# A two-stage attention and ELU kernel, rewritten: row 4p+j on partition p, fp32 loads cast on chip, one activation table, two-bank PSUM tiles, a fixed order of instructions

## Chip, cores, metric

One core of a Trainium2 chip. The metric is the device time of one execution in microseconds (us). A run has several executions, and its median is quoted. A few executions are slower (over 1.5% above the fastest of the same kernel); the ratios leave them out. The engines are PE (TensorE, the matrix engine; PEld is its weight load), DVE (VectorE), ACT (ScalarE), POOL (GpSimd) and SP (the queue engine that issues most transfers).

## The reference

```python
def _attn_ref(q, k, v, g_norm):                       # q, k, v: 8 x 8 heads x 576 x 64
    kv = np.einsum('bhsd,bhse->bhde', k, v)
    out = np.einsum('bhsd,bhde->bhse', q, kv)
    rms = np.sqrt(np.mean(out * out, axis=-1, keepdims=True) + 1e-06)
    return (out / rms * g_norm).astype(np.float32)

def _moe_ref(x, w_in, w_out):                         # x: 4608 x 512, w_in: 512 x 2048
    h = x @ w_in
    g = np.where(h > 0.0, h, np.exp(np.minimum(h, 0.0)) - 1.0)    # ELU
    return (g @ w_out).astype(np.float32)

# reference: attention, then x = heads side by side as (batch*seq, 512), then _moe_ref
```

Two large products, 4608 x 512 x 2048 and 4608 x 2048 x 512, do nearly all the arithmetic. In pieces of 128 x 128 weights and 512 moving columns they are 576 matmuls each, 1152 together. Attention is about 600 small matmuls and a row-wise norm.

## The kernel before

bf16 compute throughout. PE writes its results to tiles in a memory called PSUM; a tile of 128 x 512 fp32 is called one bank here. The software queue on POOL loads fp32 data and casts it in flight. Attention works on chunks of 128 tokens. The norm is exp(-0.5 ln(mean square + eps)) on ScalarE, and ELU is max(h, min(exp(h), 1) - 1). The compiler's scheduler orders the instructions of each engine. The parts that the argument touches:

```python
# ... one-bank PSUM tiles for both products, two of each ...
warm = const.tile([1, 1], FP32, name="warm")
nc.scalar.activation(warm, warm, AF.Exp)
nc.scalar.activation(warm, warm, AF.Ln, bias=1.0)

def load_qkv(b):                       # 128 rows a piece; runs of 64 elements
    for c in range(NCH):
        for name, src in (("k", k), ("v", v), ("q", q)):
            nc.gpsimd.dma_start(out=tiles[name][0:rows, c, :, :],
                in_=src[b, :, c*P : c*P+rows, :].rearrange("h p d -> p h d"))

def attn_chunks(b):                    # 36 chunks of 128 tokens in all
    for g in chunks:
        # ... four to eight matmuls into se_ps ...
        nc.scalar.activation(sq, se_ps, AF.Square)
        nc.vector.reduce_sum(out=ss, in_=sq, axis=X)
        nc.scalar.activation(ss, ss, AF.Ln, bias=eps_col, scale=1.0 / D)     # L185
        nc.scalar.activation(ss, ss, AF.Exp, scale=-0.5)                     # L186
        nc.vector.tensor_tensor(out=xs, in0=se_ps, in1=ss.to_broadcast(...), op=mult)
        # ... four transposes on PE, a copy to xT ...

def mlp_mm1(T):                        # T: 512 tokens
    for f in range(FC):                # 16
        # ... four matmuls into h_ps (128 x 512, one bank) ...
        nc.scalar.activation(e, h_ps, AF.Exp)                                # L222
        nc.vector.tensor_scalar(out=e, in0=e, scalar1=1.0, scalar2=1.0, op0=min, op1=subtract)
        nc.vector.tensor_tensor(out=gT[:, f, :], in0=e, in1=h_ps, op=max)    # L226

for T in range(NT):                    # 9
    # ... load, attn_pairs and attn_chunks of batch T + 2 ...
    mlp_mm1(T)
    if T > 0: mlp_mm2(T - 1)
```

## Time and profile before

442.52 us, the median of 3 runs (442.22 to 445.96).

The head of the profile page of the kernel before (span; busy time and share of each engine), then its chain that ended last, by engine and by line. The chain runs backwards from the last instruction, at each step to whatever released it:

```profile
span 442.4 us, 4765 instructions
PE 343.1 (78%) x1743; PEld 160.1 (36%) x1776; DVE 199.5 (45%) x408; ACT 265.9 (60%) x451; POOL 105.1 (24%) x128
...
PE 54%; ACT 34%; DVE 5%; POOL 3%; issue 2%; DMA 1%; ACTq 0%; POOLq 0%; DVEq 0%
PE h_ps L214 22%; PE o_ps L234 21%; ACT L185 10%; ACT L186 9%; ACT elu_e L222 5%; PE ps_shared L128 4%; PE qt_ps L147 3%; ACT sq L182 3%; DVE xs L189 2%; ACT ss L185 2%; PE ps_shared L197 2%; ACT xT L204 2%; ACT L222 2%; PE se_ps L173 2%; ACT ss L186 1%
```

PE is busy for 78% of the span (33 of its 1776 matmuls are missing from this trace: x1743 beside 1776 weight loads), yet the chain runs through it for only 54%. "ACT L185" and "ACT L186" without a tile's name are not the Ln and the Exp (those carry the name ss) but the activation-table loads ahead of them. The costliest groups of the same kernel (engine, operation, out<-in, shapes, count | busy us, mean ns of one | idle time before them):

```profile
L222 ACT ACTIVATE elu_e<-h_ps 128x512 bf16<-128x512 f32 x144 | 85.8, 596 | 77.6 <-PE h_ps L214 66.9
L226 DVE TENSOR_TENSOR gT<-elu_e,h_ps 128x512 bf16<-128x512 bf16 x144 | 98.5, 686 | 4.1
...
L185 ACT ACT_TABLE_LOAD x35 | 44.9, 1283 | 0.6
...
L186 ACT ACT_TABLE_LOAD x30 | 38.5, 1283 | 0.5
```

With six more at L222 and two at the start there are 73 loads, 73 x 1.283 = 93.7 us. Busy time by window in the kernel before (columns: length; busy us and instructions of PE, PEld, DVE, ACT and POOL; the granted TensorE clock, as a share of full speed; DMA share; GB/s):

```profile
0.00:50.00 50.00, 19.69 (x117) 10.76 (x119) 12.86 (x25) 24.80 (x43) 35.92 (x45) 1.00 1.64 155
50.00:150.00 100.00, 72.41 (x408) 35.48 (x415) 48.35 (x97) 81.48 (x139) 44.09 (x53) 0.83 1.27 82
150.00:350.00 200.00, 165.45 (x847) 76.58 (x862) 102.45 (x211) 128.20 (x217) 25.14 (x30) 0.91 0.34 39
350.00:442.00 92.00, 85.57 (x378) 37.26 (x384) 35.84 (x77) 31.47 (x53) 0.00 (x0) 0.99 0.12 46
```

From 50 to 150 us ScalarE is the busiest engine (81 of 100) and PE works at 0.83 of its clock. PE is dense at full clock only when attention is over: its last transposes start at 318.74 us, and from 319 to 350 us PE is busy for 30.7 of 31 us at a clock of 1.00. (The last window also holds the end, where PE has nothing left to do.) One chunk's norm, from the timeline of the kernel before (start us, length us, engine, line, operation):

```profile
54.98 1.28 ACT L185 ACT_TABLE_LOAD   x1
...
56.28 0.30 ACT L185 ACTIVATE ss<-ss,eps_col 128x8 f32<-128x8 f32 x1
56.60 1.28 ACT L186 ACT_TABLE_LOAD   x1
...
57.89 0.21 ACT L186 ACTIVATE ss<-ss 128x8 f32<-128x8 f32 x1
...
58.13 0.69 DVE L189 TENSOR_TENSOR xs<-se_ps,ss 128x512 bf16<-128x512 f32 x1 [2.40 <-ACT ss L186]
...
58.88 0.40 PE L197 MATMUL ps_shared<-ident,xs 128*128 128x128 bf16 x4 [2.18 <-DVE xs L189]
```

Two loads stand inside one norm: 2.57 of the 3.15 us from the first load's start to the multiply. The brackets say that VectorE stood idle for 2.40 us before its multiply, waiting for the Exp, and PE for 2.18 us before its transposes, waiting for the multiply.

### The profile page before, as it was taken

The numbers are of one execution on the slowest core, as the hardware profiler recorded it, in microseconds if no ns is written. First come the engines' busy times: TensorE is split into PE (matmuls) and PEld (weight loads), VectorE is DVE, ScalarE is ACT, GpSimd is POOL, SyncE is SP. The second block draws the span as 40 slices with busy tenths as digits, with TensorE's granted clock in tenths as the row PEclk, the third lists the DMA queues.
The fourth block names the chain that finished last, engine by engine and source line by source line (L and its number), as shares of the span: only waits on it lengthen the run. The fifth ranks groups of instructions, "written<-read, shape, count | busy, mean of one in ns | idle before, by whom it ended". The sixth has DMA issues, their size and how long they took to land.

```text
span 442.4 us, 4765 instructions
## 1 busy us (share of the span) xinstructions
PE 343.1 (78%) x1743; PEld 160.1 (36%) x1776; DVE 199.5 (45%) x408; ACT 265.9 (60%) x451; POOL 105.1 (24%) x128
## 2 busy tenths in 40 slices
PE   0443955956758947995699759995799999999994
PEld 0221422423323523452244423442344444444441
DVE  0051644643336744634564436544573636626400
ACT  2186699796797687439953894369843434424311
POOL 9949394470740280009100000000000000000000
PEclk9999988966878979999899978996899999999999
DMA  9999999590990490029600200020002002020022
GB/s 92 175 175 155 180 147 101 34 128 1 72 88 2 109 144 4 0 96 119 41 2 18 78 0 0 1 96 0 1 1 95 1 0 96 0 96 1 0 97 95
DMA packets 120040, 28.11 MB, mean 64 GB/s; under 512 B 112848, under 2 KB 114896, under 8 KB 120016
## 3 DMA queue, kind: packets, MB, share of 16 engines
q0 software_dynamic: 115104, 18.36, 59.1%
q1 hardware_dynamic: 4912, 9.44, 5.7%
q8 instruction: 14, 0.23, 0.2%
q14 instruction: 10, 0.08, 0.1%
HBM read 36.70 MB, written 9.44 MB: 104 GB/s over the span
## 4 chain that ended last, share of the span: by engine, by line
PE 54%; ACT 34%; DVE 5%; POOL 3%; issue 2%; DMA 1%; ACTq 0%; POOLq 0%; DVEq 0%
PE h_ps L214 22%; PE o_ps L234 21%; ACT L185 10%; ACT L186 9%; ACT elu_e L222 5%; PE ps_shared L128 4%; PE qt_ps L147 3%; ACT sq L182 3%; DVE xs L189 2%; ACT ss L185 2%; PE ps_shared L197 2%; ACT xT L204 2%; ACT L222 2%; PE se_ps L173 2%; ACT ss L186 1%
## 5 line engine op out<-in xcount | busy, mean ns | idle before, releaser
L214 PE MATMUL h_ps<-xT,w_in_sb 128*128 128x512 bf16 x560 | 158.4, 407 | 2.8 <-DVE gT L226 1.5
L234 PE MATMUL o_ps<-w_out_sb,gT 128*128 128x512 bf16 x559 | 149.3, 395 | 4.1 <-ACT o_sb L242 3.1
L222 ACT ACTIVATE elu_e<-h_ps 128x512 bf16<-128x512 f32 x144 | 85.8, 596 | 77.6 <-PE h_ps L214 66.9
L226 DVE TENSOR_TENSOR gT<-elu_e,h_ps 128x512 bf16<-128x512 bf16 x144 | 98.5, 686 | 4.1
L214 PEld LDWEIGHTS <-w_in_sb 128*128 128x128 bf16 x576 | 58.0, 104 | 77.3 <-issue 33.5
L234 PEld LDWEIGHTS <-gT 128*128 128x128 bf16 x576 | 57.5, 102 | 66.1 <-issue 8.0
L223 DVE TENSOR_SCALAR elu_e<-elu_e 128x512 bf16<-128x512 bf16 x144 | 42.8, 304 | 83.4 <-ACT elu_e L222 83.2
L197 PE MATMUL ps_shared<-ident,xs 128*128 128x128 bf16 x144 | 17.5, 258 | 68.0 <-DVE xs L189 51.6
L189 DVE TENSOR_TENSOR xs<-se_ps,ss 128x512 bf16<-128x512 f32 x36 | 24.8, 690 | 72.9 <-ACT ss L186 72.9
L114 POOL DMA_DIRECT2D k_sb<-in_k_dram x40 | 36.2, 906 | 90.1 <-PE ps_shared L128 54.7
L242 ACT COPY o_sb<-o_ps 128x512 f32<-128x512 f32 x31 | 18.1, 585 | 45.9 <-PE o_ps L234 43.1
L185 ACT ACT_TABLE_LOAD x35 | 44.9, 1283 | 0.6
L197 PEld LDWEIGHTS <-xs 128*128 128x128 bf16 x144 | 10.5, 111 | 87.7 <-DVE xs L189 86.6
L114 POOL DMA_DIRECT2D v_sb<-in_v_dram x40 | 36.1, 902 | 15.3 <-DMA w_out_sb<-in_moe_w_out_dram 8.2
L186 ACT ACT_TABLE_LOAD x30 | 38.5, 1283 | 0.5
L114 POOL DMA_DIRECT2D q_sb<-in_q_dram x40 | 38.3, 957 | 0.2
L128 PE MATMUL ps_shared<-v_sb,k_sb 128*128 128x128 bf16 (+1 forms) x160 | 20.9, 242 | 12.9 <-DMA v_sb<-in_v_dram 11.6
L137 ACT CAST bd_kv<-ps_shared 64x64 bf16<-64x64 f32 x46 | 9.5, 206 | 29.6 <-PE ps_shared L128 26.5
L184 DVE TENSOR_REDUCE ss<-sq 128x8 f32<-128x512 bf16 x36 | 23.8, 680 | 5.7 <-ACT sq L182 5.1
L147 PE MATMUL qt_ps<-ident,q_sb 128*128 128x128 bf16 (+1 forms) x160 | 21.2, 236 | 4.9 <-DMA q_sb<-in_q_dram 4.1
L173 PE MATMUL se_ps<-bd_kv,qT_sb 128*128 128x128 bf16 (+1 forms) x160 | 23.1, 259 | 0.5 <-ACT qT_sb L154 0.4
L204 ACT COPY xT<-ps_shared 128x512 bf16<-128x512 bf16 x31 | 17.9, 579 | 9.2 <-PE ps_shared L197 8.7
(28 smaller groups left out, 122.4 us busy)
## 6 DMA issues: line engine op xcount, KB each, us to landing
out_dram<-o_sb SPq DMA_DIRECT2D x9, 1024.0 KB, 4.3
k_sb<-in_k_dram POOLq DMA_DIRECT2D x32, 128.0 KB, 4.7
v_sb<-in_v_dram POOLq DMA_DIRECT2D x32, 128.0 KB, 4.8
q_sb<-in_q_dram POOLq DMA_DIRECT2D x32, 128.0 KB, 4.9
w_in_sb<-in_moe_w_in_dram POOLq DMA_DIRECT2D x1, 2048.0 KB, 13.2
w_out_sb<-in_moe_w_out_dram POOLq DMA_DIRECT2D x1, 2048.0 KB, 15.3
k_sb<-in_k_dram POOLq DMA_DIRECT2D x8, 64.0 KB, 4.8
v_sb<-in_v_dram POOLq DMA_DIRECT2D x8, 64.0 KB, 4.3
```

Source lines behind the costliest of these rows:

```text
L114: nc.gpsimd.dma_start(out=tiles[name][0:rows, c, :, :], in_=src[b, :, c * P : c * P + rows, :].rearrange("h p d -> p h d"),)
L128: nc.tensor.matmul(kv_ps, lhsT=k_sb[0:rows, c, 2 * p : 2 * p + 2, :], rhs=v_sb[0:rows, c, 2 * p : 2 * p + 2, :], start=(c == 0), stop=(c = ...
L147: nc.tensor.matmul(qt_ps[:, c * P : c * P + rows], lhsT=q_sb[0:rows, c, 2 * p : 2 * p + 2, :], rhs=ident[0:rows, 0:rows], is_transpose=True,)
L185: nc.scalar.activation(ss, ss, AF.Ln, bias=eps_col, scale=1.0 / D)
L186: nc.scalar.activation(ss, ss, AF.Exp, scale=-0.5)
L189: nc.vector.tensor_tensor(out=xs.rearrange("p (h e) -> p h e", h=H), in0=se_ps.rearrange("p (h e) -> p h e", h=H), in1=ss.to_broadcast([P, ...
L197: nc.tensor.matmul(p4_ps[:, j, :], lhsT=xs[:, j * P : j * P + P], rhs=ident, is_transpose=True,)
L214: nc.tensor.matmul(h_ps, lhsT=w_in_sb[:, c, f * P : f * P + P], rhs=xT[:, c, T * 512 : T * 512 + 512], start=(c == 0), stop=(c == KC - 1),)
L222: nc.scalar.activation(e, h_ps, AF.Exp)
L223: nc.vector.tensor_scalar(out=e, in0=e, scalar1=1.0, scalar2=1.0, op0=ALU.min, op1=ALU.subtract)
L226: nc.vector.tensor_tensor(out=gT[:, f, :], in0=e, in1=h_ps, op=ALU.max)
L234: nc.tensor.matmul(o_ps, lhsT=gT[:, f, ts * P : ts * P + P], rhs=w_out_sb[:, f, :], start=(f == 0), stop=(f == FC - 1),)
```

## The change

The intent: put four successive rows on one partition (row 4p+j on partition p), so that loads move runs of 1 KB on the hardware queue, in fp32, and are cast on chip; keep the one table set that holds exp and ln; halve the number of ScalarE and VectorE instructions with tiles two banks wide; and fix the order by hand, so that attention stands between matmuls of both products. The 64 rows left over of each batch of 576 form a ninth group. A cut of the diff:

```diff
+    nc.scalar.preload_act_table_set("natural_log_exp_and_others")
+    ctx.enter_context(tc.manual_schedule())
-    warm = const.tile([1, 1], FP32, name="warm")
-    nc.scalar.activation(warm, warm, AF.Exp)
-    nc.scalar.activation(warm, warm, AF.Ln, bias=1.0)
 # [cut]
+    def fetch_main(name, src, b):
+        st = stage_tile()                                   # fp32, six of them
+        nc.sync.dma_start(
+            out=st.rearrange("p (h x) -> p h x", h=H),
+            in_=src[b, :, 0:G, :].rearrange("h (p j) d -> p h (j d)", j=J))
 # [cut: tails of 64 rows, weights in four slices each; then the casts, 512 columns each, mostly on POOL]
+        def se(h):                                          # half a group: 256 tokens
+                se_ps = at_tile(FP32, 0).rearrange("p (c f) -> p c f", c=2)    # one tile for all of attention
 # [cut: eight matmuls]
+                nc.scalar.activation(sq, se_ps, AF.Square)
+                nc.vector.reduce_sum(out=ss, in_=sq.rearrange("p c (h e) -> p (c h) e", h=H), axis=AX.X)
+                nc.scalar.activation(ss, ss, AF.Ln, bias=eps_col, scale=1.0 / D)
+                nc.scalar.activation(ss, ss, AF.Exp, scale=-0.5)
+                nc.vector.tensor_tensor(out=..., in0=se_ps..., in1=ss.to_broadcast([P, 2 * H, D]), op=ALU.mult)
+        return {0: kv, 1: q_t, 2: se(0), 4: se(1), 6: x_t}  # piece by slot
+    def mm1(T, i):                                          # eight matmuls, two f at once
+        h_ps = ps_m1.tile([P, 2, G], FP32, name="h_ps", tag="mm1")
 # [cut]
+        nc.scalar.activation(e, h_ps, AF.Exp)
 # [cut: min and subtract, max, on 1024 columns, in rest()]
+    cast_all(1)
+    for i in range(8):
+        mm1(0, i)()                                         # group 0: first product alone
+    fetch(2)
+    at = attention(1)
+    for i, n in ((0, None), (1, 1), (2, 0), (3, 2)):        # six of its eight units of the second
+        mm2(0, i)
+        if n is not None:
+            at[n]()
+    mm2(0, 4)
+    at[4]()
+    mm2(0, 5)
+    at[6]()
+    late = [6, 7]
+    for T in range(1, NT):                                  # NT = 9 groups of 512 tokens
 # [cut: casts of T+1, loads of T+2]
+        for i in range(8):
+            rest = mm1(T, i)
+            if T == 1:
+                if i < 2:
+                    mm2(0, late[i])
+            else:
+                mm2(T - 1, i)
+            rest()
+            if T + 1 < NT and i in at:
+                at[i]()
+    for i in range(8):
+        mm2(NT - 1, i)
```

## The prediction

> **What bounds it now.** (1) To about 11 us nothing but loads (busy time by window: PE 1.0 us of 11). (2) 50-150 us: PE busy is 72 of 100 us at a granted clock of 0.80-0.86, ScalarE 81 of 100. The page lists 73 activation-table loads of 1283 ns, 93.7 us; the chain that ended last gives ScalarE 34%, the Ln and Exp lines 18%, nearly all of it table loads. (3) From 350 us PE is dense at clock 1.00: 49 matmuls of 512 columns take 10.74 us on the chain, so 0.216 us each. The 1152 large matmuls are thus worth 248 us at full clock, in a span of 442.
>
> **Removed.** All table loads but one. The Trainium skill (ScalarE: Activation LUTs, "Table sets: the hidden batching unit") says one set holds both exp and ln; this trace shows the alternation and its 1283 ns. Also removed: 115,104 small packets on the software queue, whose issues cost POOL 110 us. Attention: 9 groups of 512 tokens in place of 36 of 128.
>
> **Added.** fp32 loads and on-chip casts. The stores' packets (2 KB) went at 9.44 MB in 5.7% of 442 us, 374 GB/s; for 1-2 KB loads I estimate 250-370 GB/s, so 12-14 us a batch, hidden after the start. POOL casts: no line shows one; from its 128-column memset (205 ns) and select (309 ns) I estimate 0.5-0.9 us per 512 columns, 14 a batch, about 10 us of 33, hidden; at the start 50 of them, 35 us.
>
> **Moved.** ELU on 1024 columns: Exp about 1.03 us, min/sub 0.44 (from 304 ns at 512 and 2343 at 8192), max 1.22; 2.9 us with handoffs. With two buffers, eight matmuls (1.73 us) alone run one pair-tile per 2.3 us, but interleaved with eight of the second product the chain has 3.5 us of slack: PE-bound. Within a group Square-reduce-Ln-Exp-multiply takes about 4.5 us against 6.9 us of matmuls placed between its ends: hidden. ScalarE then works about 17 of 33 us, VectorE 20.
>
> **Sum.** Small matmuls: 60-95 ns start to start in dense stretches at full clock, so 68 a group are about 5 us.
> - Until the first product starts (load q, k, v; one attention alone, serial): 37 us (32-48).
> - First product of group 0, alone: 18.
> - Six units of its second product with attention 1, too little work to hide the chain: 22.
> - Group 1: 26.
> - Groups 2-7: 6 x 33 = 198.
> - Group 8, no attention: 28.
> - Last second product, alone: 14; copy and store: 4.
>
> Total 347 us. PE stays dense, so the clock should rise to about 0.97. The skill (TensorE: Matmul & The Clock Gate, "The HAM clock gate") lets the clock fall after idle windows of about 3.4 us; the trace agrees in direction (0.80 where gaps of 2-4 us lie, 1.00 where dense).
>
> Predicted 347 us, 332 to 369. Chances: faster 0.97, same 0.02, slower 0.01.
>
> **What would show each step.** Table loads: 1. Exp about 1.03 us on 128x1024. PE busy over 95% of each window from group 2 to the end, clock 1.00 there, groups 33 us apart. First large matmul at 32-48 us. Chain of waits: PE over 80%.
>
> **What would make it wrong.** POOL casts twice my estimate (port shared with VectorE) would stall group 1's attention by 10-20 us. Loads at 180 GB/s would add 10-20 us at the start. A chain I call hidden may show: 2 us per group are 14 us. Small matmuls at 150 ns (the cold rate) would add 4 us a group.

## The result

351.97 us, the median of 4 runs (350.18 to 352.89), against 444.24 us before (442.22 to 449.66, 4 runs); the ratio is 0.7903, interval 0.7843 to 0.7962. 449.66 is 1.7% above the fastest, and without it the median is the 442.52 quoted above. A ratio here is the mean time of one kernel's fast runs over that of the other's of the same rounds, so not quite the ratio of the medians quoted.

The page head, the chain and the groups of the changed kernel, to be read against those of before:

```profile
span 351.1 us, 4399 instructions
PE 303.7 (86%) x1760; PEld 151.2 (43%) x1760; DVE 180.8 (52%) x207; ACT 145.9 (42%) x200; POOL 82.3 (23%) x144
...
PE 78%; DVE 8%; ACT 7%; DMA 4%; issue 1%; SPq 1%; DVEq 0%
...
L285 ACT ACTIVATE elu_e<-h_ps 128x1024 bf16<-128x1024 f32 x72 | 73.4, 1021 | 57.2 <-PE h_ps L277 57.2
L291 DVE TENSOR_TENSOR gT<-elu_e,h_ps 128x1024 bf16<-128x1024 bf16 x72 | 87.9, 1221 | 7.5
...
L132 POOL CAST q_bf<-st 128x512 bf16<-128x512 f32 x36 | 21.5, 633 | 138.6 <-DMA st<-in_q_dram 118.9
```

ScalarE's busy time fell by 120 us, of which 72 loads are 92. PE's fell by 39 us although it does the same products. Part of this is the clock: in the mean 0.921 was granted before and 0.982 now.

Busy time by the stages that the prediction had named (start; first product of group 0; six units of its second product with attention 1; group 1; group 2 to the last matmul):

```profile
0.00:36.80 36.80, 9.40 (x68) 6.99 (x69) 10.59 (x15) 7.71 (x14) 16.74 (x34) 1.00 0.98 321
36.80:57.57 20.77, 17.01 (x64) 6.65 (x64) 11.82 (x14) 8.28 (x8) 15.43 (x26) 1.00 1.11 298
57.57:79.52 21.95, 15.82 (x118) 8.53 (x117) 9.32 (x9) 7.45 (x14) 8.17 (x14) 0.99 0.60 165
79.52:111.25 31.73, 27.61 (x148) 12.88 (x148) 17.78 (x20) 13.18 (x19) 14.15 (x24) 0.85 0.57 156
111.25:345.50 234.25, 233.69 (x1364) 116.18 (x1363) 131.33 (x150) 108.73 (x147) 27.77 (x47) 1.00 0.27 83
```

The last line is the point of the rewrite: for 234 us PE is busy for all but 0.6 us at full clock, while VectorE works for 131 and ScalarE for 109. The kv matmuls (k times v, the first matmuls of a batch's attention) of successive batches, from PE's timeline, give the period of a group:

```profile
115.42 2.01 PE L177 MATMUL at<-v_bf,k_bf 128*128 128x128 bf16 x20
...
147.68 2.01 PE L177 MATMUL at<-v_bf,k_bf 128*128 128x128 bf16 x20
```

32.26 us: 128 large matmuls at 0.216 us are 27.6, and the 68 small ones take the other 4.6. Nothing else is left in a group. Of the 47.4 us in which PE is not busy (351.1 - 303.7), 41.4 lie before 111.25 us.

| stage | predicted us | measured us |
|---|---|---|
| to the first large matmul | 37 | 36.8 |
| first product of group 0 | 18 | 20.8 |
| six units with attention 1 | 22 | 22.0 |
| group 1 | 26 | 31.7 |
| groups 2 to 7 (111.25 to 304.02) | 198 | 192.8 |
| group 8 (to 331.66) | 28 | 27.6 |
| last product (to 345.5) | 14 | 13.8 |
| copy, store, end | 4 | 5.6 |
| sum | 347 | 351.1 |

(331.66 is 331.44 us, where the last 65 large matmuls start on the timeline, plus one of 0.216 us.)

### The profile page after: what moved, and what is told of

It is laid out like the page before. It is cut to its first block, busy times and chain, and to the rows that moved or that the text cites. A ratio compares the mean times of both kernels' runs of the same rounds, so it can differ in the third digit from the quotient of the medians.

```text
span 351.1 us, 4399 instructions
## 1 busy us (share of the span) xinstructions
PE 303.7 (86%) x1760; PEld 151.2 (43%) x1760; DVE 180.8 (52%) x207; ACT 145.9 (42%) x200; POOL 82.3 (23%) x144
## 4 chain that ended last, share of the span: by engine, by line
PE 78%; DVE 8%; ACT 7%; DMA 4%; issue 1%; SPq 1%; DVEq 0%
PE h_ps L277 33%; PE o_ps L305 33%; PE at L177 5%; DMA st<-in_v_dram 4%; DVE gT L291 3%; PE at L252 2%; ACT elu_e L285 2%; PE at L210 2%; PE at L192 2%; DVE xs L236 2%; DVE ss L229 2%; DVE elu_e L288 1%; ACT sq L227 1%; ACT xT L262 1%; ACT qT L200 1%
## 5 line engine op out<-in xcount | busy, mean ns | idle before, releaser
L277 PE MATMUL h_ps<-xT,w_in_sb 128*128 128x512 bf16 x576 | 141.7, 390 | 8.8 <-DVE gT L291 5.7
L285 ACT ACTIVATE elu_e<-h_ps 128x1024 bf16<-128x1024 f32 x72 | 73.4, 1021 | 57.2 <-PE h_ps L277 57.2
L291 DVE TENSOR_TENSOR gT<-elu_e,h_ps 128x1024 bf16<-128x1024 bf16 x72 | 87.9, 1221 | 7.5
L288 DVE TENSOR_SCALAR elu_e<-elu_e 128x1024 bf16<-128x1024 bf16 x72 | 34.6, 480 | 93.3 <-ACT elu_e L285 93.1
L132 POOL CAST q_bf<-st 128x512 bf16<-128x512 f32 x36 | 21.5, 633 | 138.6 <-DMA st<-in_q_dram 118.9
L229 DVE TENSOR_REDUCE ss<-sq 128x16 f32<-128x1024 bf16 x18 | 21.9, 1219 | 21.8 <-ACT sq L227 21.8
L236 DVE TENSOR_TENSOR xs<-at,ss 128x1024 bf16<-128x1024 f32 x18 | 22.0, 1225 | 11.3 <-ACT ss L233 11.3
L227 ACT ACTIVATE sq<-at 128x1024 bf16<-128x1024 f32 x18 | 18.5, 1026 | 18.2 <-PE at L210 15.6
L177 PE MATMUL at<-v_bf,k_bf 128*128 128x128 bf16 (+1 forms) x160 | 17.2, 232 | 8.2 <-ACT qT L200 8.2
L132 POOL CAST v_bf<-st 128x512 bf16<-128x512 f32 x28 | 16.9, 641 | 8.4 <-DMA st<-in_v_dram 8.4
L252 PE MATMUL at<-ident,xs 128*128 128x128 bf16 x144 | 10.3, 229 | 6.7 <-DVE xs L236 6.7
```

Source lines behind the costliest of these rows:

```text
L132: eng.tensor_copy(out=out_, in_=in_)
L177: nc.tensor.matmul(kv_ps[:, p, :], lhsT=k_sb[0:rows, c, 2 * p : 2 * p + 2, :], rhs=v_sb[0:rows, c, 2 * p : 2 * p + 2, :], start=(c == 0), ...
L229: nc.vector.reduce_sum(out=ss, in_=sq.rearrange("p c (h e) -> p (c h) e", h=H), axis=AX.X)
L236: nc.vector.tensor_tensor(out=st["xs"][:, 2 * h : 2 * h + 2, :].rearrange("p c (h e) -> p (c h) e", h=H), in0=se_ps.rearrange("p c (h e) - ...
L277: nc.tensor.matmul(h_ps[:, a, :], lhsT=w_in_sb[:, c, f * P : f * P + P], rhs=x[:, c, :], start=(c == 0), stop=(c == KC - 1),)
L291: nc.vector.tensor_tensor(out=gT[T][:, 2 * i : 2 * i + 2, :], in0=e, in1=h_ps, op=ALU.max)
```

## The experiments

A total that fits says nothing about which part of a rewrite earned it. The first eight runs take the parts one at a time; the last four use what came out. All twelve gave correct results. "Before" was run in the same rounds each time (medians 443.99 to 445.2; two of them hold one slow execution). The runs went over four chips: the control, the filled, the one-bank and the scheduler's-order run shared one. The fast medians of before on the four, 442.92 to 444.53 us, lie 1.6 us apart, so a difference between runs on two chips is uncertain by about that much.

| run | median us | ratio to before | interval |
|---|---|---|---|
| changed kernel, control | 351.28 | 0.7912 | 0.7877 to 0.7948 |
| before + one table set | 357.88 | 0.8040 | 0.7998 to 0.8082 |
| changed, two table sets | 359.23 | 0.8088 | 0.8029 to 0.8147 |
| changed, software loads | 365.88 | 0.8223 | 0.8182 to 0.8264 |
| changed, products in blocks | 397.71 | 0.8939 | 0.8897 to 0.8982 |
| changed, gaps filled | 350.22 | 0.7876 | 0.7842 to 0.7910 |
| changed, one-bank tiles | 350.80 | 0.7887 | 0.7845 to 0.7928 |
| changed, scheduler's order | 338.52 | 0.7614 | 0.7572 to 0.7657 |
| scheduler's order, two table sets | 359.08 | 0.8078 | 0.8005 to 0.8151 |
| new opening (3 fast of 4) | 342.59 | 0.7729 | 0.7666 to 0.7792 |
| new opening, shorter start | 338.10 | 0.7621 | 0.7571 to 0.7671 |
| the last, scheduler's order | 331.78 | 0.7470 | 0.7426 to 0.7514 |

### One table set in the kernel before

```diff
-    warm = const.tile([1, 1], FP32, name="warm")
-    nc.vector.memset(warm, 0.0)
-    nc.scalar.activation(warm, warm, AF.Exp)
-    nc.scalar.activation(warm, warm, AF.Ln, bias=1.0)
+    nc.scalar.preload_act_table_set("natural_log_exp_and_others")
```

> The kernel before with the one table set that holds both exp and ln loaded at the start, nothing else changed. Theory A (mine): the 73 loads of 1283 ns were on the chain only in the crowded part, and behind them stands the same schedule, with one-bank tiles whose exp-min-max chain holds PE: table loads fall from 73 to 1, ScalarE's busy time from 266 to about 174 us, the time from 444 to 400-415 us. Rival B: the loads were the whole story: the 18% of the chain goes and the time falls to 355-370 us.

Measured: 357.88 us. Theory A was wrong and the rival right: this one line is worth 86.6 us, and all the rest of the rewrite then adds 6.6 us (357.88 to the control's 351.28). The head of its page:

```profile
span 356.7 us, 4723 instructions
PE 317.1 (89%) x1776; PEld 150.6 (42%) x1776; DVE 200.3 (56%) x407; ACT 172.8 (48%) x377; POOL 105.0 (29%) x128
...
PE 70%; DMA 11%; POOL 7%; DVE 6%; ACT 3%; issue 2%; POOLq 0%; DVEq 0%
```

The chain's share on ScalarE falls from 34% to 3%. The spans of the two profiles differ by 85.7 us (442.4 and 356.7), and they split in two: time in which PE was not busy fell from 99.3 to 39.6 us (442.4 - 343.1 and 356.7 - 317.1), 59.7 us; PE's busy time for the same work fell by 26.0 us, with the granted clock up from 0.921 to 0.998. (The 33 matmuls missing from the trace of before, at 0.216 us each, could move up to 7 us from the first part to the second.) The waits that went are PE's before the transposes of the normalised tile (ps_shared <- ident, xs): for xs and for the copy that empties the tile, they sum to 68.0 us before (51.6 and 16.4) and to 5.8 here (5.0 and 0.8). So the 92.4 us of removed loads (72 x 1.283) paid twice: fewer waits, and fewer slow matmuls. My theory had taken the tiles of one bank for the next limit, and PE is at 49.4 to 49.8 of every 50 us from 100 to 300 us with those tiles.

### Two table sets in the changed kernel

```diff
-    nc.scalar.preload_act_table_set("natural_log_exp_and_others")
```

> The changed kernel without the preload of the joint set, so that Ln and Exp alternate between sets again: about 36 to 55 loads of 1283 ns, 46 to 70 us more on ScalarE. Theory A: the fixed interleave hides nearly all of it from group 2 on (4.4 us of chain in 6.9 us of slack), so group period stays within 1 us of 32.3; the serial parts (start, attention 1, group 1) pay about 2.6 us per half, 6 halves: 366-378 us. Rival B: table loads cost what they take: 398-422 us.

Measured: 359.23 us, 8 us over the control, with 37 loads back. Theory A's mechanism held, its size was too high (it expected 366 to 378). The kv matmuls of successive batches in this kernel:

```profile
120.00 2.01 PE L176 MATMUL at<-v_bf,k_bf 128*128 128x128 bf16 x20
152.26 2.01 PE L176 MATMUL at<-v_bf,k_bf 128*128 128x128 bf16 x20
184.65 2.01 PE L176 MATMUL at<-v_bf,k_bf 128*128 128x128 bf16 x20
```

The period is 32.26 and then 32.39 us, against 32.26: in the steady groups the loads cost next to nothing. The 4.6 us by which the 120.00 lies after the 115.42 of the changed kernel's first profile are paid earlier, where too little stands beside the norm: 1.0 up to the kv matmuls of attention 1 (65.28 against 64.25), 1.0 more up to those of group 1 (88.20 against 86.17) and 2.6 in group 1. That is nearly all of the 5.1 us by which these two profiled executions differ (357.95 and 352.89). The medians, from two chips, differ by 8; what the slower executions pay besides is not shown.

### Scheduler's order, two table sets

```diff
-    ctx.enter_context(tc.manual_schedule())
-    nc.scalar.preload_act_table_set("natural_log_exp_and_others")
```

> The changed kernel with the order left to the scheduler and, besides, without the preload, so that its 36 to 54 table loads are back. It asks why 73 loads cost 87 us in the kernel before and 36 cost 8 us in the changed one. Theory A: the wide tiles do it (half the loads, and chains that are started half as often): 343-352 us, 5 to 13 us over the scheduler's 338.5. Rival B: the fixed order hid them, and a scheduler that does not count on loads lets PE wait for each: 365 us or more.

Measured: 359.08 us, 20.6 us over the same kernel with one set (338.52), between the two theories. From group 3 on, its kv matmuls come every 34.2 us (145.52, 179.69, 213.87, 248.04 us on its timeline) in place of 32.26, so here each group does pay, about 1.9 us. About half is paid before: the 145.52 already lies 10.6 us after the 134.94 of the one-set partner, and the two profiles end 19.9 us apart. Set side by side, what a table load cost in time:

| kernel | loads | their time, us | what they cost, us |
|---|---|---|---|
| before (narrow tiles, scheduler) | 73 against 1 | 92.4 | 86.6 |
| changed, scheduler's order | 37 against 1 | 46.2 | 20.6 |
| changed, fixed order | 37 against 1 | 46.2 | 8.0 |

(The costs are differences of medians; the one-set partners are the run with one table set in the kernel before, the run in the scheduler's order and the control.) The wide tiles halve the number of loads, and what remains costs less per load; the fixed order hides most of it besides. The traces show where the cost lands: the loads add 46.6 us to PE's waits for the normalised tile in the kernel before (51.6 against 5.0), 13.6 in the scheduler's order (23.9 against 10.3) and 5.1 in the fixed order (19.6 against 14.5). Why a load in the kernel before cost nearly its full time is not settled by a run of its own. An estimate from the profile's durations: per 128 tokens the serial norm before is 0.60 + 0.68 + 1.28 + 0.30 + 1.28 + 0.21 + 0.69 = 5.0 us, 36 times 181 us; in wide tiles with the loads 1.03 + 1.22 + 2.57 + 0.31 + 0.22 + 1.22 = 6.6 us, 18 times 118 us. The loads also stand among ELU's Exps on ScalarE's timeline (the Exp at 58.01 us comes after the loads at 54.98 and 56.60). That the crowding does it is argued, not shown; wide tiles and hardware loads came together in this comparison.

### Software loads in the changed kernel

```diff
     def fetch_main(name, src, b):
-        st = stage_tile()
-        nc.sync.dma_start(out=st..., in_=src[b, :, 0:G, :].rearrange("h (p j) d -> p h (j d)", j=J))
+        t = qkvp.tile([P, J + 1, H, D], BF16, name=f"{name}_bf", tag=name)
+        for j in range(J):
+            nc.gpsimd.dma_start(out=t[:, j, :, :],
+                in_=src[b, :, 0:G, :].rearrange("h (p j) d -> p j h d", j=J)[:, j, :, :])
 # the tails likewise; no casts of q, k and v on chip
```

> The changed kernel with q, k and v loaded by the software queue with the cast in flight, as before, into the same tiles; no fp32 staging and no POOL casts of them. Theory A: the load path matters at the start only: one batch takes about 29-32 us of all 16 engines (261 us for 8 batches and the weights in the kernel before), so the first large matmul moves from 37 to about 55-65 us and group 1's and 2's attention wait; the steady groups (32.3 us) just keep up: 375-400 us. Rival B: small packets do not matter once the rest is interleaved: within 2% of 352.

Measured: 365.88 us, 14.6 us over the control. The first large matmul, in this kernel and in the changed one:

```profile
50.86 6.31 PE L280 MATMUL h_ps<-xT,w_in_sb 128*128 128x512 bf16 x16 [0.84 <-DVE xT L262]
```
```profile
36.80 5.99 PE L277 MATMUL h_ps<-xT,w_in_sb 128*128 128x512 bf16 x16 [0.84 <-DVE xT L259]
```

The first large matmul comes 14.1 us later. By the kv matmuls of group 2 the lag is 12.5 us (127.92 against 115.42), so 1.6 us are won back in between; the steady period is again 32.26 us (127.92, 160.18, 192.44 us on its timeline), and the two profiled executions end 12.7 us apart (365.62 and 352.89). So the load path matters at the start alone, as theory A said; its waits in groups 1 and 2 did not come, and its range was too high. "Within 2%" also falls: the two ratios differ by 3.9% and their intervals lie apart.

### Products in blocks

```diff
         for i in range(8):
             rest = mm1(T, i)
-            mm2(T - 1, i)
             rest()
             if T + 1 < NT and i in at:
                 at[i]()
+        for i in range(8):
+            mm2(T - 1, i)
```

(Group 1 is treated likewise with its two units.)

> The changed kernel with both products of a group in blocks: all eight units of the first product (with the attention pieces still between them), then all eight of the second. Theory A: the interleave is what hides the exp-min-max chain: the first product then runs at the rate of group 0's, about 2.5 us a unit in place of 1.73, and the attention chain has half the matmuls to hide behind: 6 to 10 us a group, 400-425 us in all, with PE waiting for VectorE's max and for the normalised tile. Rival B: two-bank tiles with two buffers suffice by themselves: under 360 us.

Measured: 397.71 us, 46 us over the control and 2 us below theory A's range. A group now takes 39.5 us (kv at 150.88, 190.37, 229.92), 7.2 us more than 32.26. PE's timeline shows what it is spent on:

```profile
161.98 1.89 PE L277 MATMUL h_ps<-xT,w_in_sb 128*128 128x512 bf16 x8 [0.38 <-DVE gT L291]
164.96 0.61 PE L210 MATMUL at<-bd_kv,qT 128*128 128x128 bf16 x8 [1.09 <-DVE xs L236]
166.61 3.75 PE L277 MATMUL h_ps<-xT,w_in_sb 128*128 128x512 bf16 x16 [1.05 <-DVE gT L291]
171.45 1.05 PE L252 MATMUL at<-ident,xs 128*128 128x128 bf16 x16 [1.09 <-DVE xs L236]
...
174.83 13.98 PE L305 MATMUL o_ps<-w_out_sb,gT 128*128 128x512 bf16 x64
```

In the first product PE waits again and again, for VectorE's max (gT), which frees a tile, and for the normalised tile (xs); with a wait for the copy of q these add up to 6.1 us in the group from 150.88 us. Then 64 matmuls of the second product run without a gap, when VectorE and ScalarE have little to do. Interleaving the two products is thus necessary in this kernel. It was there before, too, made by the scheduler.

### One-bank tiles

```diff
-    ps_m1 = ... tile_pool(name="ps_m1", bufs=2, ...)    # tiles of two banks
+    ps_m1 = ... tile_pool(name="ps_m1", bufs=4, ...)    # tiles of one bank
+        # Exp, min and subtract, max for each of the two f alone, on 512 columns
```

> The changed kernel with one-bank tiles for the first product (four buffers of one bank, Exp, min/sub and max on 512 columns). Theory A: from group 2 on PE bounds, so more fixed cost on ScalarE (+12 us) and VectorE (+19 us) is hidden; group 0's first product gains from the finer pipeline or loses from VectorE's 8 us: 348-356 us, same within 2%. Rival B: the two-bank tiles carry part of the gain: 362 us or more.

Measured: 350.80 us, the control's 351.28 within the intervals. With one table set and the fixed order, the width of the first product's tiles does not matter; the steady period is 32.26 us here as well. ScalarE is busy for 154.5 us in place of 145.6 and VectorE for 198.7 in place of 181.2, and this is hidden. So this part of the change, halving the instructions of ELU, earned nothing measurable (attention's tiles stayed two banks wide).

### Gaps filled

```diff
     mm2(0, 4)
+    fill(11)          # matmuls of 512 columns into a free tile of the first product
     at[4]()
     mm2(0, 5)
+    fill(11)
     at[6]()
+    fill(4)
```

> The changed kernel with 26 needless large matmuls (their results are never read) put where PE waits in attention 1: 11 before the second half, 11 before the transposes, 4 after. Theory A: the clock fell for group 1 (0.84 granted, eight matmuls in 3.87 us in place of 1.89) because PE idled for about 6 of the 9.5 us before it. With the gaps filled the clock stays at 1.0 there, and group 1 is 2.5 to 3.5 us shorter: 348-350 us, that is 2 to 3.5 us under the control. Rival B: the low clock comes from elsewhere (loads at full rate in that window, or chance): the stretch stays slow and the time is the control's or above it.

Measured: 350.22 us against 351.28, just outside theory A's range and 1.1 us under the control where it had expected 2 to 3.5; the intervals overlap, so the timing alone is unclear. The profiles are not. PE's timeline of the control, at the turn to group 1 and at a later row of group 1, then of the filled kernel (L372 is the filler):

```profile
73.46 0.61 PE L210 MATMUL at<-bd_kv,qT 128*128 128x128 bf16 x8 [2.53 <-DVE xs L236]
73.90 1.89 PE L305 MATMUL o_ps<-w_out_sb,gT 128*128 128x512 bf16 x8
78.28 1.05 PE L252 MATMUL at<-ident,xs 128*128 128x128 bf16 x16 [2.48 <-DVE xs L236]
80.17 3.87 PE L277 MATMUL h_ps<-xT,w_in_sb 128*128 128x512 bf16 x8 [0.84 <-DVE xT L259]
83.83 3.01 PE L305 MATMUL o_ps<-w_out_sb,gT 128*128 128x512 bf16 x8
...
102.42 5.30 PE L277 MATMUL h_ps<-xT,w_in_sb 128*128 128x512 bf16 x16 [1.05 <-DVE gT L291]
```
```profile
75.35 2.54 PE L372 MATMUL f_ps<-xT,w_in_sb 128*128 128x512 bf16 x11
78.00 1.05 PE L252 MATMUL at<-ident,xs 128*128 128x128 bf16 x16
78.89 1.03 PE L372 MATMUL f_ps<-xT,w_in_sb 128*128 128x512 bf16 x4
79.89 0.59 PE L277 MATMUL h_ps<-xT,w_in_sb 128*128 128x512 bf16 x2
81.04 1.46 PE L277 MATMUL h_ps<-xT,w_in_sb 128*128 128x512 bf16 x6 [0.55 <-ACT xT L262]
82.33 1.89 PE L305 MATMUL o_ps<-w_out_sb,gT 128*128 128x512 bf16 x8
```

The long durations (3.87 and 3.01 in place of 1.89; 5.30 for 16, where two rows of eight take 3.96 us in the filled kernel) are gone. The granted clock in group 1 is 1.00 in place of 0.85, and group 1 takes 28.9 us (79.89 to 108.83) in place of 31.5 (80.17 to 111.69). The mean clock of all five filled executions is 0.990 to 1.000, that of the six of the control 0.981 to 0.986. The loads in group 1 were not fewer (172 GB/s against 157), so rival B falls. So the gaps did lower the clock. They explain 2.6 us of group 1's loss; that the rest comes from six units of the first product without the second beside them is argued from PE's waits there (for VectorE's max and for the normalised tile, between 92 and 108 us), not tested.

### Scheduler's order

```diff
-    ctx.enter_context(tc.manual_schedule())
```

> The changed kernel with the order of instructions on each engine left to the compiler's scheduler, as in the kernel before, in place of the fixed order. Theory A: the scheduler works with costs that are not the chip's and bunches small work, as the trace of before shows (large matmuls in blocks of 35 and 49, waits of 2-4 us for the normalised tile): 365-390 us. Rival B: the written order is just what the scheduler finds: within 1% of 352.

Measured: 338.52 us, 12.8 us faster than the control. Both theories fell: the order by hand is the slower one. The kv matmuls of the same batch (4) start at 134.94 us here and at 147.68 in the changed kernel:

```profile
134.94 2.01 PE L175 MATMUL at<-v_bf,k_bf 128*128 128x128 bf16 x20
...
167.20 2.01 PE L175 MATMUL at<-v_bf,k_bf 128*128 128x128 bf16 x20
```

They are 12.7 us apart, and both then follow at 32.26 us, so from there on the two run alike. The whole difference lies before, 10.2 us of it before the kv matmuls of batch 3 (105.22 against 115.42). It is the opening, where the scheduler moved units of group 0's second product into the waits of its first product, and of group 1's into group 1's; the hand-written order had left those waits empty.

### A new opening, by hand

```diff
+    fetch(1)
     for s in range(4):
         fetch_w_out(s)
-    fetch(1)
 # [cut: casts of batch 1 likewise ahead of those of w_out]
-    for i in range(8):
-        mm1(0, i)()
-    # ... six units mm2(0, i) with attention 1 between them ...
+    slot = {0: 1, 2: 0, 3: 2, 5: 4, 7: 6}
+    for i in range(8):
+        mm1(0, i)()
+        if i in slot:
+            at[slot[i]]()                 # attention 1 between the units of the first product
 # [cut: all of mm2(0, i) then stands in group 1, as in any later group]
```

> The changed kernel, fixed order, with another opening: batch 1 is loaded and cast before w_out, attention 1 stands between the units of group 0's first product, and all of group 0's second product stands between the units of group 1's first, as in every later group. Theory A: the loss against the scheduler's order (351 to 338.5 us) lies all in the opening, where attention 1 has too little beside it: large work is moved to where PE waits, group 2 starts at 94-98 us in place of 111, the time is 332-340 us, the granted clock stays at 1.0 after 45 us. Rival B: the opening is bound by the loads (4.2 MB of w_out then come later), and the gaps only move: 345 us or more.

Measured: 342.59 us, the median of its three fast executions (343.08 with the fourth), 8.7 us better than the control and 2.6 us worse than theory A's range. The clock did not stay at 1.0: its mean was 0.986 to 0.990 in the three. The profile that should show where the 2.6 us went fell on the fourth, an odd execution of 1102 us (see the last section), so this run does not tell; the next one's profile does.

The same with a shorter start (the edit is against the run above):

```diff
+        else:                                          # batch 0
+            fetch_tail("k", k, b, nc.scalar)
+            fetch_tail("v", v, b, nc.scalar)
 # [cut]
     cast("k", 0, [V])
+    at0[1]()                                           # transposes of q
     cast("v", 0, [V, A])
 # [cut]
+    at0[4](ps_m1.tile([P, 2, G], FP32, name="h_ps", tag="mm1"))    # second half in a tile of its own
```

> The last one, with a shorter start besides: the two 64-row tails of batch 0 are issued from ScalarE's queue after the main loads, the transposes of q come before the cast of v, and the second half of attention 0 takes a PSUM tile of the first product's, so that the two halves' chains overlap. Theory A: v is cast 3-4 us earlier, the kv product no longer waits for the copy of q (1 us), and the overlap saves about 3 us: first large matmul at 28-31 us in place of 36.8, the time 6-9 us under the last one, 325-332 us. Rival B: the weights' loads then bound the first product: less than 3 us.

Measured: 338.10 us, 4.5 us under the last one; theory A had expected 6 to 9, the rival less than 3. The first large matmul of the first product came at 31.8 us (28 to 31 expected, 36.8 before). Group 0's first product with attention 1 then took 29.9 us (31.80 to 61.67). PE waits 2.8 us for the last copy at its end and for VectorE's max several times, and after these gaps the timeline shows slow matmuls twice more: 15 in 5.30 us from 52.68 (granted clock 0.67) and 8 in 3.11 us from 64.57 (0.58). It looks as if too little work stood beside attention 1, again; that is argued, not tested.

And this kernel with its order left to the scheduler:

```diff
-    ctx.enter_context(tc.manual_schedule())
```

> The kernel with the new opening and the shorter start (338.1 us in the fixed order), its order left to the scheduler: a try for the fastest version. Theory A: what the scheduler won over the fixed order (351 to 338.5 us) it won in the opening, which is now written by hand; from group 2 on both orders keep PE at 100%, so nothing is left to win but some of the waits of attention 1 (about 6 us) and the clock that falls with them: 332-338 us. Rival B: the scheduler undoes the hand-made opening, moving attention ahead of the large work: 340 us or more.

Measured: 331.78 us in 6 runs, the fastest version; theory A's range held it. The head of its page:

```profile
span 329.6 us, 4392 instructions
PE 298.6 (91%) x1760; PEld 150.0 (45%) x1760; DVE 179.5 (54%) x207; ACT 147.1 (45%) x200; POOL 81.3 (25%) x144
```

PE is idle for 31.0 us in all (329.6 - 298.6), most of it before its first large matmul at 30.9 us, where it is busy for 9.7.

## Why the prediction was right, point by point

- The total: 347 predicted, 352 measured, inside 332 to 369. The stages were built from durations of the old trace and nearly all came out: Exp on 1024 columns 1.03 predicted and 1.02 measured, max 1.22 and 1.22, min and subtract 0.44 and 0.48, a POOL cast 0.5 to 0.9 and 0.63, loads 250 to 370 GB/s and 321 over the first 36.8 us, a steady group 33 and 32.3.
- "PE busy over 95% of each window from group 2 to the end, clock 1.00": 233.69 of 234.25 us at 1.00. "Table loads: 1": one. "Chain of waits: PE over 80%" missed, at 78%, and at 71% in the control's profile of the same kernel, so this share moves between executions.
- The term that was mis-sized most: "Group 1: 26", measured 31.7. The filled run shows 2.6 us of it to be the clock, lowered by PE's waits in attention 1. The prediction had foreseen those waits (22 us for the six units, measured 22.0) and had not carried their effect on the clock into the next stage. The rest of the miss goes, as argued above, with the first product without the second beside it.
- "First product of group 0, alone: 18", measured 20.8: its first 16 matmuls took 5.99 us, where 16 x 0.216 + 0.17 is 3.6, so 2.4 us of the 2.8 are again a low rate after idle time. (The clock column reads 1.00 in that stretch, so here the durations show the low rate and the column does not.)
- These were partly offset by "Groups 2-7: 6 x 33 = 198", measured 192.8: the sum, 4 us off, is better than its terms, and that is luck.
- Not in the prediction, and wrong when I wrote it down before the first experiment: which part earns the gain. I held one-bank tiles and their chain for the limit behind the table loads. The one-line run gave 86.6 of the 93 us by itself. So the right total does not vouch for the parts: the prediction listed the loads as one removal among several. The gains do not add: the rest of the rewrite with two table sets also gives 85 us (444 to 359). Either cure is nearly enough, since both end at the same limit, PE with 0.216 us for each of 1152 matmuls.
- The fixed order, a named part of the change, costs 12.8 us as written, all before the kv matmuls of batch 4. Nothing in the prediction compared it with what the scheduler would do.

The Trainium skill carried two steps. ScalarE: Activation LUTs, section "Table sets: the hidden batching unit", says that one named set holds exp and ln, "1 TABLE_LOAD"; this agrees, with 73 loads before and 1 after. TensorE: Matmul & The Clock Gate, Part 1, "The HAM clock gate", says that activity releases a throttle and idling brings it back; this agrees, 0.85 in group 1 after gaps and 1.00 when they are filled, though after shorter gaps than the page's figure (last section).

What stays open: why a table load cost nearly its full time in the kernel before and a fifth of it in the fixed order (the traces show that PE waits for the normalised tile, not which part of the rewrite shortens that wait); and which of wide tiles and hardware loads makes the scheduler's version tolerate 37 loads.

## What to carry to other kernels

Look first for activation-table loads on the chain of waits: a set that holds all functions in use is one line, and here it was worth as much as a rewrite. When a large change is measured, take its parts singly, in both directions: alone on the old kernel, and missing from the new one, because gains that end at the same limit do not add. Compare an order written by hand with the scheduler's before keeping it, and look at the opening, where the steady pattern has no partner yet.

## What the Trainium skill lacked or had wrong

- TensorE: Matmul & The Clock Gate, Part 1 and the table of goals: the page lets the clock fall after one idle window of about 3.4 us and asks for "No PE-idle gaps >~3µs". These figures do not cover what happened here. In the run with two table sets the granted clock was 0.50 from 103.56 us (eight small matmuls in 1.01 us in place of 0.61) after a gap of 2.37 us; before that gap PE had waited only 0.38 us since 97 us. In the control it was 0.66 from 102.42 us after gaps of 1.09 and 1.05 us with eight small matmuls between. The filled kernel has these same two gaps and kept 1.00, so the length of a gap alone does not decide it. The fall at 80.17 us is a weaker case: the 16 matmuls between its last two gaps (2.48 and 0.84 us) are transposes, and without them PE is idle for 4.4 us.
- The same page, caveat on the HAM trace: "stuck at K=1/4 for 50+µs". One of the four executions of the kernel with the new opening took 1102 us, and its profile shows every large matmul, from the first at 40.62 us to the end, at about 0.82 us (6.56 us between one set of eight and the next), 3.8 times the 0.216 of the others, while ScalarE's busy time was unchanged (150 us). The result lists a clock of 1.00 for it, and the page of the profile has no clock row. The other three took 342.0 to 343.6 us. Whether this is the state that the page means is not shown; it lasted a thousand us.
- The same page, Part 2, "Back-to-back issue gap": it gives about 131 ns a matmul of 512 columns as a sustained figure. Pairs of weight load and matmul run at 0.216 us start to start at full clock, in every dense stretch; the page's own 2.4 GHz formula fits, the 131 ns does not.
- ScalarE: Activation LUTs, "What ACT_TABLE_LOAD costs": it adds a drain of about 1380 ns to the 1283 of each load. The loads took 1283 ns here, and the timeline of before leaves no room for the drain: a load starts 0.02 us after the end of the Ln (56.28 + 0.30, then 56.60), and the next activation 0.01 us after the load (57.89).
- GPSIMD Engine Reference, 4.1: it calls one-input work "roughly line-rate" without a figure for a cast. An fp32 to bf16 cast of 128 x 512 took 633 ns on POOL, 422 on VectorE and 618 on ScalarE in the changed kernel.
